# A gated mix of linear attention and a dense layer: dense units first, features laid out head by head, KV accumulated tile by tile

## The chip, the cores and the metric

One core of one Trainium2 chip. The metric is the device time of one execution in microseconds (us); lower is better. "Span" is the time from the first to the last instruction in a profile; in the runs below the time is 1.8 us longer than the span of the same execution. Engines are called by their names in the profile: PE (TensorE; PEld is its weight load), DVE (VectorE), ACT (ScalarE), POOL (GpSimd) and SP (which only issues transfers). A profile marks executions "slow" or "fast"; here one core runs alone, so "slow" only means over 1.5% above the fastest execution of that kernel.

## The reference, cut to what matters

```python
# x: 2048 x 512 (bf16).  H = 32 heads of 16.  DFF = 1376.
q, k, v  = split(x @ wqkv)                       # per head
pq, pk   = q @ w_phi[h], k @ w_phi[h]            # 16 x 16 per head
phi      = concat([softmax(p), softmax(-p)])     # 32 features per head
kv, z    = sum_s phi_k^T v, sum_s phi_k
a        = ((phi_q kv) / (phi_q z + 1e-6)) @ wo
b        = relu(x @ w1) @ w2
g        = sigmoid(sum(x * gate_w))
return g * a + (1 - g) * b
```

## The kernel before

Rows of x come in 16 tiles of 128. w_phi is folded into the q and k weights at the start (`WqP`, `WkP`), which needs those weights transposed. A *dense unit* is one product group of the dense layer: four 512-column matmuls and a relu; there are 44. The program order on PE is: fold, 16 tiles with the 44 units spread between them, a KV stage, and a final stage of 16 rounds (query product, B = hidden x w2, A = heads x wo). Softmax sums and reciprocals are DVE's, the scaling by them POOL's, the exponentials ACT's.

```python
# start: the transposed loads, one queue, wqkv first (SP); plain loads through POOL's software queue
S_wqk.op(lambda: sync.dma_start_transpose(out=WQKT, in_=A_wqkv[:, 0:2 * D]))
for q in range(NCH):
    S_xT[q].op(... sync.dma_start_transpose(out=XO[:, :, q*512:(q+1)*512], in_=x2[q*512:(q+1)*512, :]))
S_wv.op(lambda: pool.dma_start(out=WV[:, :, :], ...))
S_w1.op(lambda: pool.dma_start(out=W1[:, :, :], ...))
...
# PE, per tile: q and k features, V, and the gate as a one-column matmul
for dt in range(NDT):
    pe.matmul(PS[:, 0, :], lhsT, WqP[:, dt, :], ...); pe.matmul(PS[:, 1, :], lhsT, WkP[:, dt, :], ...)
for dt in range(NDT):
    pe.matmul(PS[:, 2, :], lhsT, WV[:, dt, :], ...);  pe.matmul(PS[:, 3, m:m + 1], lhsT, GW[:, dt, :], ...)
...
# PE, KV stage after all tiles: per group of 128 features, 16 tiles of (128 columns + 1 column for z)
pe.matmul(PS[:, kb, kc:kc + P], lhsT, VS[:, m, t*P:(t+1)*P], ...)
pe.matmul(PS[:, zb, zc:zc + 1], lhsT, ONES[:, 0:1], ...)
...
# PE, final stage: query product of 8 x 136 columns
pe.matmul(PS[:, bank, c0:c0 + P + 8], lhsT, KVNZ[:, g, :], ...)
```

The softmax here doesn't subtract the row's maximum and nothing guards it: scores larger than these inputs give would overflow.

## Time and profile before

Median 178.93 us of 3 runs (177.81 to 180.07). The head of the profile's page, with the chain of work that ended last:

```profile
span 176.5 us, 2702 instructions
...
PE 155.9 (88%) x1072; PEld 81.9 (46%) x1088; DVE 109.0 (62%) x197; ACT 70.0 (40%) x98; POOL 55.3 (31%) x49
...
PE 88%; DMA 5%; issue 2%; ACT 2%; DVE 1%
```

PE is on the chain for 88% of the span, so nearly every microsecond saved on PE should show. The window view of the same kernel, cut at five stages (each line: the stretch, its length, then busy time and number of instructions of PE, PEld, DVE, ACT, POOL, then the granted PE clock, the busy share of the DMA engines and their GB/s):

```profile
0.00:18.20 18.20, 3.61 (x33) 3.38 (x34) 3.90 (x10) 3.35 (x5) 5.30 (x14) 0.99 1.01 210
18.20:101.80 83.60, 82.38 (x423) 37.17 (x432) 71.34 (x96) 55.62 (x77) 49.01 (x35) 0.98 0.42 86
101.80:113.00 11.20, 10.50 (x257) 10.42 (x257) 5.38 (x27) 0.00 (x1) 0.99 (x1) 1.00 0.15 28
113.00:173.70 60.70, 59.40 (x361) 30.90 (x368) 27.71 (x64) 10.99 (x16) 0.00 (x0) 1.00 0.27 68
173.70:176.50 2.80, 0.00 (x0) 0.00 (x0) 0.72 (x1) 0.00 (x0) 0.00 (x0) 1.00 0.14 47
```

| stage | us | PE busy |
|---|---|---|
| start | 18.2 | 3.6 |
| tiles and dense units | 83.6 | 82.4 |
| KV | 11.2 | 10.5 |
| final stage | 60.7 | 59.4 |
| tail | 2.8 | 0 |

So the start is, but for the short tail, the only stage in which PE is mostly idle. The timeline (start, duration, engine, line, operation) says what it waits for: the transposed load of wqkv, issued at 0.75 and landed at 10.36.

```profile
0.75 3.98 SPq L226 DMA_TRANSPOSE HTW<-in_A_wqkv_dram  x1
...
10.36 1.89 PE L431 MATMUL PS<-Wbd,HTW 128*128 128x128 bf16 x16 [10.36 <-DMA HTW<-in_A_wqkv_dram]
```

The next lines, from the timeline of DVE and POOL inside one tile, show a place where DVE never idles. From one reciprocal (65.51) to the next (69.92) a tile takes DVE 4.41 us, and its small product at 67.56 (32 elements) ends at 68.11, just after POOL's multiply ends at 68.07:

```profile
65.51 0.55 DVE L363 RECIPROCAL SC<-ZB 128x64 f32<-128x64 f32 x1
...
66.14 1.93 POOL L279 TENSOR_TENSOR FM<-FM,SC 128x1024 bf16<-128x1024 bf16 x1 [2.20 <-DVE SC L363]
...
67.56 0.55 DVE L369 TENSOR_TENSOR SC<-ZB,SC 128x32 f32<-128x32 f32 x1
...
69.92 0.55 DVE L363 RECIPROCAL SC<-ZB 128x64 f32<-128x64 f32 x1
```

That the small product waits for POOL is plainer in the first tile, where POOL's multiply started late: there the same 32 elements took 1.75 us, and ended (28.72) just after POOL (28.66) once more.

```profile
26.72 1.94 POOL L279 TENSOR_TENSOR FM<-FM,SC 128x1024 bf16<-128x1024 bf16 x1
26.97 1.75 DVE L369 TENSOR_TENSOR SC<-ZB,SC 128x32 f32<-128x32 f32 x1
```

In the kernel before DVE's 4.41 us do not bind: a tile with its units takes PE 83.6 / 16 = 5.2 us.

### The profile page before, as it was taken

Reading aid. Unit: us, or ns where it says so; the run is one execution under the profiler, and the core shown is the slowest. Engines: PE = TensorE matmul, PEld = TensorE weight load, DVE = VectorE, ACT = ScalarE, POOL = GpSimd, SP = SyncE. Lnnn points to the kernel's source line nnn. Section 1 sums busy time; section 2 is a strip of 40 time slices with the busy share of each in tenths; the row PEclk is TensorE's granted clock in tenths of the full one; section 3 lists DMA queues with packets and bytes.
Section 4 is the critical chain, followed back from the end, with each engine's and each line's share of the span. In section 5 each row is a group of like instructions: output and inputs, shape, how many; then the busy total and the mean of one; then the engine's idle time right before and its main releaser. Section 6 shows DMA issues by size and latency. Waiting matters only on the chain.

```text
span 176.5 us, 2702 instructions
## 1 busy us (share of the span) xinstructions
PE 155.9 (88%) x1072; PEld 81.9 (46%) x1088; DVE 109.0 (62%) x197; ACT 70.0 (40%) x98; POOL 55.3 (31%) x49
## 2 busy tenths in 40 slices
PE   0061899999999999999999899799999999999993
PEld 0061344444444444444444399655555555555541
DVE  1223079988989889888899954444554445544431
ACT  2004067766666767666666700002111121111230
POOL 8300047666565446665566620000000000000000
PEclk9999699999999999999999999999999999999999
DMA  5999949933333320323333330041322232322321
GB/s 124 261 182 265 241 96 323 164 59 59 59 63 59 61 49 16 61 58 59 59 59 59 59 63 4 4 83 36 89 60 63 61 89 77 76 60 59 80 68 59
DMA packets 41467, 15.58 MB, mean 88 GB/s; under 512 B 38528, under 2 KB 40592, under 8 KB 41456
## 3 DMA queue, kind: packets, MB, share of 16 engines
q1 hardware_dynamic: 40352, 11.54, 32.8%
q0 software_dynamic: 1104, 3.88, 7.5%
q8 instruction: 8, 0.13, 0.3%
q14 instruction: 3, 0.02, 0.0%
HBM read 3.88 MB, written 2.10 MB: 34 GB/s over the span
## 4 chain that ended last, share of the span: by engine, by line
PE 88%; DMA 5%; issue 2%; ACT 2%; DVE 1%
PE PS L488 22%; PE PS L554 21%; PE PS L459 8%; PE PS L468 8%; PE PS L457 8%; PE PS L562 8%; PE PS L512 6%; DMA HTW<-in_A_wqkv_dram 5%; PE PS L539 4%; ACT WkP L295 1%; PE PS L431 1%; PE PS L437 1%; DVE OTM L412 0%; DVE OSB L421 0%; ACT HTW L317 0%
## 5 line engine op out<-in xcount | busy, mean ns | idle before, releaser
L488 PE MATMUL PS<-XO,W 128*128 128x512 bf16 (+1 forms) x171 | 40.3, 379 | 0.3
L554 PE MATMUL PS<-W,HTW 128*128 128x512 bf16 (+1 forms) x170 | 40.0, 379 | 0.3
L279 POOL TENSOR_TENSOR FM<-FM,SC 128x1024 bf16<-128x1024 bf16 x16 | 30.9, 1928 | 26.3 <-DVE SC L363 26.3
L327 ACT ACTIVATE TFA<-PS,GT 128x512 bf16<-128x512 f32 x16 | 11.0, 687 | 59.2 <-PE PS L562 42.0
L421 DVE SCALAR_TENSOR_TENSOR OSB<-PS,OMG,TFA 128x512 bf16<-128x512 f32 x16 | 12.0, 751 | 31.8 <-PE PS L554 20.8
L317 ACT ACTIVATE HTW<-PS 128x512 bf16<-128x512 f32 (+1 forms) x44 | 26.3, 598 | 7.5 <-PE PS L488 7.5
L457 PE MATMUL PS<-WqP,XO 128*128 128x512 bf16 x62 | 24.5, 395 | 4.2 <-issue 4.2
L309 ACT ACTIVATE FM<-PS 128x1024 bf16<-128x1024 f32 x16 | 16.4, 1023 | 22.6 <-PE PS L459 22.6
L459 PE MATMUL PS<-WkP,XO 128*128 128x512 bf16 x64 | 25.2, 393 | 0.1
L554 PEld LDWEIGHTS PS<-W,HTW 128*128 128x128 bf16 (+1 forms) x176 | 16.7, 98 | 17.5
L488 PEld LDWEIGHTS PS<-XO,W 128*128 128x128 bf16 (+1 forms) x176 | 15.4, 99 | 19.8 <-ACT HTW L317 3.8
L360 DVE TENSOR_REDUCE ZB<-FM 128x64 f32<-128x1024 bf16 x16 | 19.5, 1218 | 3.1 <-ACT FM L310 3.1
L364 DVE TENSOR_REDUCE ZB<-FM 128x64 f32<-128x1024 bf16 x16 | 18.6, 1161 | 0.0
L355 DVE CAST VS<-PS 128x512 bf16<-128x512 f32 x16 | 11.0, 686 | 10.8 <-PE PS L471 10.8
L285 POOL TENSOR_TENSOR FM<-FM,SC 128x512 bf16<-128x512 bf16 x16 | 16.9, 1055 | 2.0
L468 PE MATMUL PS<-WV,XO 128*128 128x512 bf16 x62 | 17.3, 377 | 0.0
L310 ACT ACTIVATE FM<-PS 128x1024 bf16<-128x1024 f32 x16 | 16.3, 1018 | 0.0
L562 PE MATMUL PS<-WO,XO 128*128 128x512 bf16 x63 | 16.2, 378 | 0.1
L412 DVE TENSOR_TENSOR OTM<-PS,RDEN 128x256 bf16<-128x256 f32 x32 | 12.1, 420 | 0.6
L457 PEld LDWEIGHTS PS<-WqP,XO 128*128 128x128 bf16 x64 | 6.4, 100 | 12.4 <-issue 5.3
L539 PE MATMUL PS<-KVNZ,PHQ 128*128 128x136 bf16 x128 | 10.0, 223 | 1.5 <-DVE OTM L412 0.9
L512 PE MATMUL PS<-VS,FM 128*128 128x128 bf16 x128 | 10.5, 216 | 0.8 <-ACT EG L320 0.8
(44 smaller groups left out, 134.7 us busy)
## 6 DMA issues: line engine op xcount, KB each, us to landing
out_dram<-OSB SPq DMA_DIRECT2D x16, 128.0 KB, 1.9
W<-in_B_w_dram POOLq DMA_DIRECT2D x1, 1376.0 KB, 12.7
W<-in_B_w_dram POOLq DMA_DIRECT2D x1, 1280.0 KB, 6.8
WV<-in_A_wqkv_dram POOLq DMA_DIRECT2D x1, 512.0 KB, 6.9
WO<-in_A_wo_dram POOLq DMA_DIRECT2D x1, 512.0 KB, 8.8
PHQ<-FM SPq DMA_TRANSPOSE x16, 3.1
XO<-OTM SPq DMA_TRANSPOSE x16, 2.4
W<-in_B_w_dram POOLq DMA_DIRECT2D x1, 96.0 KB, 6.5
```

What stands on the lines that cost most here:

```text
L279: POp.op(lambda m=m, b=b: pool.tensor_tensor(fmk(m).rearrange("p (g d) -> p g d", d=DH), fmk(m).rearrange("p (g d) -> p g d", d=DH), SC[:, ...
L317: ACp.op(lambda kt=kt, c=c, M=M, hb=hb: act.activation(HT[0:M, kt, c * 512:(c + 1) * 512], PS[0:M, hb, :], ACT.Relu), ev=f"rl{u}")
L360: VEp.op(lambda b=b, m=m: vec.tensor_reduce(ZB[:, b, 2 * H:4 * H], fmk(m).rearrange("p (g d) -> p g d", d=DH), AX.X, ALU.add), ev=f"zk{m}")
L364: VEp.op(lambda b=b, buf=buf: vec.tensor_reduce(ZB[:, b, 0:2 * H], fmq(buf).rearrange("p (g d) -> p g d", d=DH), AX.X, ALU.add), ev=f"zq{m}")
L457: PEp.op(lambda lhsT=lhsT, dt=dt, st=st, sp=sp: pe.matmul(PS[:, 0, :], lhsT, WqP[:, dt, :], start=st, stop=sp))
L459: PEp.op(lambda lhsT=lhsT, dt=dt, st=st, sp=sp: pe.matmul(PS[:, 1, :], lhsT, WkP[:, dt, :], start=st, stop=sp), ev=(f"pqk{m}" if sp else N ...
L468: PEp.op(lambda lhsT=lhsT, dt=dt, st=st, sp=sp: pe.matmul(PS[:, 2, :], lhsT, WV[:, dt, :], start=st, stop=sp), ev=(f"v{m}" if sp else None))
L488: PEp.op(lambda lhsT=lhsT, dt=dt, c=c, hb=hb, M=M: pe.matmul(PS[0:M, hb, :], lhsT, XO[:, dt, c * 512:(c + 1) * 512], start=(dt == 0), stop ...
L512: PEp.op(lambda lhsT=lhsT, kb=kb, kc=kc, m=m, t=t: pe.matmul(PS[:, kb, kc:kc + P], lhsT, VS[:, m, t * P:(t + 1) * P], start=(m == 0), stop ...
L539: PEp.op(lambda lhsT=lhsT, bank=bank, c0=c0, g=g, sg=sg: pe.matmul(PS[:, bank, c0:c0 + P + 8], lhsT, KVNZ[:, g, :], start=(sg == 0), stop= ...
L554: PEp.op(lambda kt=kt, M=M, m=m, B_b=B_b: pe.matmul(PS[:, B_b, :], HT[0:M, kt, m * P:(m + 1) * P], W2[0:M, kt, :], start=(kt == 0), stop=( ...
L562: PEp.op(lambda t=t, m=m, A_b=A_b: pe.matmul(PS[:, A_b, :], XO[:, t, m * P:(m + 1) * P], WO[:, t, :], start=(t == 0), stop=(t == NG - 1)))
```

## The change

The intent: fill PE's idle start with dense units, and take work off PE. The first 512 rows of x are loaded plainly and transposed on PE (after seven warm-up products), the first 8 dense units run while wqkv's transposed load is under way, and 3 more after the fold. Features are laid out head by head, so that a group of 128 features belongs to only 4 heads: products with V then need 64 columns plus one of ones, those with KV 68. KV is accumulated in PSUM three tiles behind the exponentials. The gate weights ride as a spare row of the last dense unit. Eleven units are kept for the time after the last tile. The diff, cut to its core:

```diff
+        WQKT = PHQ[:, :, S - 512:S]          # transposed wqkv in space for late query features
+        XS = OT[:, :, 0:512]
+        for j in range(4):                   # x0, plain, on two hardware queues
+            p.dma(("sp", "act")[j // 2], ... e.dma_start(out=XS[:, j, :], in_=x2[j * P:(j + 1) * P, :]), ...)
+        w1cuts = [0, 256, 512, 1024, DFF]
+        for i in range(4):                   # w1 in four cuts, ahead of wqkv
+            p.dma(("act", "act", "sp", "sp")[i], ... W1[:, :, a:b] ...)
+        p.wait("pool", ["x01", "x03"])
+        p.wait("sp", ["x03"])
+        p.dma("pool", ... out=WV[:, :, :] ...)                                # software queue
+        p.dma("sp", lambda e: e.dma_start_transpose(out=WQKT, in_=A_wqkv[:, 0:2 * D]), "wqk", ev="wqk")
+        for c in range(1, NCH):
+            p.dma("sp", ... e.dma_start_transpose(out=XT[:, :, c * 512:(c + 1) * 512], ...))
         ... cut ...
+        # per tile: q, k, V (no gate column); V waits for the cast of the tile before: one V bank
+                after=((["wv"] + ([f"cv{m - 1}"] if m else [])) if dt == 0 else ()), ...
+        # KV, three tiles behind: 8 products of 65 columns per tile
+                    PS[:, 6 + g // 4, (g % 4) * GW:(g % 4) * GW + 65],
+                    FM[:, b, 1, g * P:(g + 1) * P], VS[:, b, g, 0:65],
+        # query product: 8 products of 68 columns per tile
+                    PHQ[:, g, m * P:(m + 1) * P], KVNZ[:, g, :], start=True, stop=True),
-                        PS[:, 3, m:m + 1], lhsT, GW[:, dt, :], start=st, stop=sp),
-                    PS[:, kb, kc:kc + P], lhsT, VS[:, m, t * P:(t + 1) * P],
-                    PS[:, zb, zc:zc + 1], lhsT, ONES[:, 0:1],
-                                PS[:, bank, c0:c0 + P + 8], lhsT, KVNZ[:, g, :],
         ... cut ...
+        for kt in range(8):
+            hunit(0, kt)
+        pre()                                # the fold
+        for kt in range(8, KT):
+            hunit(0, kt)
+        # then 16 tiles with 22 units between them, 11 late units, the final stage
```

## The prediction

> **What bounds it now.** TensorE: the chain of waits gives PE 88% of the 176.5 us span, and the granted clock is 0.990. The windows and the timeline show five stages: start 18.2 us (10.4 of it waiting for the transposed load of wqkv, then products and copies); tiles plus dense units 83.6 (PE busy 82.4); KV 11.2; final stage 60.7 (PE busy 59.4); tail 2.8. Times run 2.4 us over the span.
>
> **Costs read from the timeline.** A 512-column matmul takes 0.2165 us in a stream, a 136-column one 0.059, a gate column adds 0.025 to 0.03, a KV pair (128+1 columns) 0.081 to 0.088. I estimate 0.04 for a 65- or 68-column matmul.
>
> **What the change does.**
> - Start: chunk 0 of x is loaded plainly and transposed on PE, so dense units fill the wait for wqkv. First unit at 6.5 us, wqkv still at 14, first tile at 19, but 11 of 44 units (9.5 us) are then done.
> - Gate column: 64 matmuls go, about 2 us.
> - KV: 256 matmuls in an own stage (11.2) become 128 short ones among the tiles, about 5 us.
> - Query product: 128 x 0.059 = 7.5 becomes about 5.
>
> **What takes over in the middle.** Per tile PE then needs 12 x 0.2165 + 22/16 units x 0.866 + 0.3 = 4.1 us on average (5.2 now). VectorE keeps its work per tile. The product of the scale waits for GpSimd: it ends 0.04 us after GpSimd's 1.93 us multiply. The Trainium skill, "SBUF — State Buffer", section "Who interferes with whom", says a tensor_tensor with both inputs in SBUF contends with GpSimd; this trace agrees. Where VectorE never idled (reciprocal at 65.51 to the next at 69.92) a tile took 4.41 us. Bank 2 is single: V of the next tile waits for VectorE's cast, in program order behind the previous tile's softmax sums. So VectorE can lag by little more than a us, and the tiles run at about 4.4 us, not 4.1: 16 tiles about 70 us. The exponentials' chain (1.93 + 1.94 us) stays just below. The 11 late units hide the last KV products: another 8.5 us.
>
> **Sum.** Start 19 + tiles and late units 79 (98) + final stage 16 x (2.38 + 0.87 + 0.3) = 57, plus about 2 us where it begins (first B waits for the last relu; first A waits for the transpose of the first numerator, 2.4 us) + tail 3.7 (A is last now) = 160.5 span, plus 2.4: **163 us**, 80% range 158 to 168.5. Faster by over 2% 0.96, within 0.03, slower 0.01.
>
> **What would show it right.** First dense matmul before 8 us, first tile at 17 to 21; tile period 4.3 to 4.6 us with VectorE over 90% busy in the tiles and PE waiting for the cast before V; no KV stage of its own; final period 3.5 to 3.6 us with PE over 95%; PE idle about 1 us at the final stage's start.
>
> **What would make it wrong.** VectorE less in the way: 4.1 us per tile, 158. Interleaved 16-element runs slowing the exponentials or GpSimd's multiply: a GpSimd or ScalarE period over 4.6 would add 3 to 10 us. GpSimd waits for the last x chunk (about 27 us) before it multiplies tile 0; counted as absorbed. A of the final stage now waits for a transpose only two tiles ahead, with 0.9 us of slack; a slower landing would stall every tile. wqkv could land 3 us later.

## The result, and the profile after

The changed kernel ran at a median of 170.57 us (4 runs, 168.54 to 172.73) against 178.39 us for the kernel before (4 runs). The ratio of fast runs is 0.953, 95% interval 0.944 to 0.962. Ratios in this document are the mean time of one kernel's fast runs over that of the other's of the same rounds, so not quite the ratio of the medians quoted. The kernel is faster, by about half of what was predicted, and 163 us with its range up to 168.5 missed.

The profile that came with this result fell in a slow execution (172.73 us). The kernel was therefore run again unedited (label `again`), and that profile is of a fast one (169.01 us). Its page:

```profile
span 167.2 us, 2373 instructions
...
PE 152.6 (91%) x919; PEld 72.3 (43%) x919; DVE 103.9 (62%) x174; ACT 72.9 (44%) x102; POOL 54.7 (33%) x48
...
PE 47%; DVE 33%; DMA 9%; issue 6%; ACT 2%; ACTq 1%; DVEq 0%
```

PE's busy time fell by only 3.3 us, though many products are gone: warm-up products (3.2 us) and transposes came in, and parts of the start ran at half clock. The chain changed its make-up: DVE, 1% of it before, is 33% of it now. The windows, cut at the first tile, the end of the dense units, and the last product:

```profile
0.00:26.30 26.30, 19.49 (x99) 9.37 (x100) 6.46 (x23) 9.26 (x15) 4.61 (x13) 0.87 1.03 188
26.30:105.60 79.30, 76.43 (x453) 35.60 (x452) 69.35 (x101) 52.64 (x71) 50.09 (x35) 1.00 0.35 80
105.60:163.90 58.30, 56.70 (x368) 27.35 (x368) 27.32 (x50) 10.74 (x16) 0.00 (x0) 1.00 0.30 71
163.90:167.20 3.30, 0.00 (x0) 0.00 (x0) 0.75 (x1) 0.26 (x1) 0.00 (x0) 0.83 0.12 40
```

| stage | predicted | fast run | off by |
|---|---|---|---|
| start, to the first tile | 19 | 26.3 | +7.3 |
| tiles and late units | 79 | 79.3 | +0.3 |
| final stage with its beginning | 57 + 2 | 58.3 | -0.7 |
| tail | 3.7 | 3.3 | -0.4 |
| time over span | 2.4 | 1.8 | -0.6 |
| time | 163 | 169.0 | +6.0 |

Each stage behind the first tile came out within a microsecond, though in the middle two errors cancelled (see the account at the end). The miss is in the start. Its timeline in the fast run (SPq is the issue on SP's queue):

```profile
4.24 14.46 SPq L170 DMA_TRANSPOSE PHQ<-in_A_wqkv_dram  x1
...
9.30 3.45 PE L223 MATMUL PS<-XT,W 128*128 128x512 bf16 x8 [3.22 <-DMA W<-in_B_w_dram]
14.87 7.04 PE L223 MATMUL PS<-XT,W 128*128 128x512 bf16 x24 [2.12 <-DMA W<-in_B_w_dram]
21.75 2.17 PE L253 MATMUL PS<-Wbd,PHQ 128*128 128x128 bf16 x32
...
26.34 0.38 PE L273 MATMUL PS<-WqP,XT 128*128 128x512 bf16 x1
```

Two kinds of losses are there. Units wait twice for w1 (3.22 and 2.12 us). And the products are slow for a while after each gap: 8 products in 3.45 us are 0.43 us each, while a stream at full clock takes 0.2165. The Trainium skill, "TensorE: Matmul & The Clock Gate", section "What's actually happening", says that an idle PE falls back to half its clock and needs a window of some 3.4 us of work to recover; this trace agrees with both. The view by windows of one microsecond gives a granted clock of 0.50 between 10 and 12 and between 16 and 19 us, and the windows beside them (0.54 and 0.75; 0.95 and 0.84) make each stretch some 3.4 us long. The second stretch begins a microsecond after PE had gone back to work at full pace, so the clock follows a gap with a delay.

The transposed load of wqkv, which the prediction worried about, held up nothing in this run: it landed at 20.9 us, while PE was at its units until 21.75. The chain that ended last, cut to the start, goes through w1's second cut instead, which was issued at 2.15 and landed at 14.82:

```profile
2.15 12.67 DMA W<-in_B_w_dram
...
14.87 7.04 PE PS L223 x24
```

In the slow run the start is longer, and there the fold itself waits for wqkv:

```profile
8.07 3.46 PE L223 MATMUL PS<-XT,W 128*128 128x512 bf16 x8 [2.19 <-DVE Wbd L200]
13.10 5.35 PE L223 MATMUL PS<-XT,W 128*128 128x512 bf16 x24 [1.57 <-DMA W<-in_B_w_dram]
23.06 3.59 PE L253 MATMUL PS<-Wbd,PHQ 128*128 128x128 bf16 x32 [4.61 <-DMA PHQ<-in_A_wqkv_dram]
...
30.15 0.38 PE L273 MATMUL PS<-WqP,XT 128*128 128x512 bf16 x1
```

Between these two executions the whole difference of 3.7 us lies before the first tile. That the scatter of the changed kernel over 4 us comes from there too is likely, but only these two were profiled. The loads behind it, from the list of transfers of the fast run (last figure: us from issue to landing):

```profile
WV<-in_A_wqkv_dram POOLq DMA_DIRECT2D x1, 512.0 KB, 13.1
...
PHQ<-in_A_wqkv_dram SPq DMA_TRANSPOSE x1, 16.7
```

The transposed load of wqkv takes 16.7 us (18.2 in the slow run), not the 9.6 us of before; it lands at 20.9 us. In the middle of the kernel DVE is as busy as foretold: it goes from one reciprocal to the next in 48.98 - 44.61 = 4.37 us with no idle time, and the cast of V (47.14) waits in program order behind the previous tile's sums:

```profile
44.61 0.55 DVE L297 RECIPROCAL SC<-ZB 128x64 f32<-128x64 f32 x1
...
46.66 0.56 DVE L304 TENSOR_TENSOR SC<-ZB,SC 128x32 f32<-128x32 f32 x1
47.14 0.68 DVE L291 CAST VS<-PS 128x512 bf16<-128x512 f32 x1
...
48.98 0.55 DVE L297 RECIPROCAL SC<-ZB 128x64 f32<-128x64 f32 x1
```

### The profile page after: what moved, and what is told of

Same layout as the page of the kernel before. It is cut to its first block, busy times and chain, and to the rows that moved or that the text cites. A ratio compares the mean times of both kernels' runs of the same rounds, so it can differ in the third digit from the quotient of the medians.

```text
span 170.9 us, 2373 instructions
## 1 busy us (share of the span) xinstructions
PE 153.3 (90%) x919; PEld 73.3 (43%) x919; DVE 104.2 (61%) x174; ACT 73.3 (43%) x102; POOL 54.6 (32%) x48
## 4 chain that ended last, share of the span: by engine, by line
PE 44%; DVE 32%; DMA 14%; issue 6%; ACT 2%; ACTq 0%; DVEq 0%
PE PS L384 21%; DMA PHQ<-in_A_wqkv_dram 11%; DVE ZB L294 9%; DVE ZB L299 9%; PE PS L223 9%; PE PS L394 8%; DVE VS L291 5%; DVE SC L302 3%; DMA OT<-in_A_x_dram 2%; PE PS L253 2%; PE PS L360 2%; DVE SC L297 2%; DVE SC L304 2%; DMA OT<-OTM 1%; ACT FM L288 1%
## 5 line engine op out<-in xcount | busy, mean ns | idle before, releaser
L223 PE MATMUL PS<-XT,W 128*128 128x512 bf16 (+1 forms) x176 | 44.3, 397 | 3.8 <-DVE Wbd L200 2.2
L384 PE MATMUL PS<-W,HT 128*128 128x512 bf16 (+1 forms) x176 | 40.6, 379 | 0.9 <-ACT EG L347 0.8
L288 ACT ACTIVATE FM<-PS 128x1024 bf16<-128x1024 f32 x32 | 31.0, 1021 | 20.6 <-PE PS L273 20.6
L237 ACT ACTIVATE HT<-PS 128x512 bf16<-128x512 f32 (+1 forms) x44 | 26.2, 598 | 16.9 <-PE PS L223 16.8
L223 PEld LDWEIGHTS PS<-XT,W 128*128 128x128 bf16 (+1 forms) x176 | 17.9, 104 | 25.5 <-issue 2.9
L273 PE MATMUL PS<-WqP,XT 128*128 128x512 bf16 x64 | 24.3, 380 | 1.0 <-ACT FM L288 0.6
L273 PE MATMUL PS<-WkP,XT 128*128 128x512 bf16 x64 | 24.2, 379 | 0.0
L384 PEld LDWEIGHTS PS<-W,HT 128*128 128x128 bf16 (+1 forms) x176 | 16.2, 97 | 18.7 <-issue 1.2
L299 DVE TENSOR_REDUCE ZB<-FM 128x64 f32<-128x1024 bf16 x16 | 18.6, 1161 | 0.0
L311 POOL TENSOR_TENSOR FM<-FM,SC 128x512 bf16<-128x512 bf16 x16 | 16.9, 1055 | 2.0
L279 PE MATMUL PS<-WV,XT 128*128 128x512 bf16 x64 | 16.5, 380 | 1.1 <-DVE VS L291 0.9
L394 PE MATMUL PS<-WO,OT 128*128 128x512 bf16 x64 | 16.4, 378 | 1.0 <-DMA OT<-OTM 1.0
L370 DVE TENSOR_TENSOR OTM<-PS,RDEN 128x512 bf16<-128x512 f32 x16 | 11.1, 692 | 0.5
```

The lines of the kernel that those rows point to most:

```text
L223: p.op("pe", lambda e, c=c, kt=kt, M=M, dt=dt, bank=bank: e.matmul(PS[0:M, bank, :], W1[:, dt, kt * P:kt * P + M], XT[:, dt, c * 512:(c + ...
L237: p.op("act", lambda e, c=c, kt=kt, Mr=Mr, bank=bank: e.activation(HT[0:Mr, kt, c * 512:(c + 1) * 512], PS[0:Mr, bank, :], ACT.Relu), afte ...
L273: p.op("pe", lambda e, m=m, dt=dt, which=which, W=W: e.matmul(PS[:, which, :], XT[:, dt, m * P:(m + 1) * P], W[:, dt, :], start=(dt == 0), ...
L279: p.op("pe", lambda e, m=m, dt=dt: e.matmul(PS[:, 2, :], XT[:, dt, m * P:(m + 1) * P], WV[:, dt, :], start=(dt == 0), stop=(dt == NDT - 1) ...
L288: p.op("act", lambda e, o=fm5[:, :, :, s, :], i=src, s=s: e.activation(o, i, ACT.Exp, scale=(1.0 if s == 0 else -1.0)), after=[f"qk{m}"] + ...
L299: p.op("dve", lambda e, b=b: e.tensor_reduce(ZB[:, b, 0:64], FM[:, b, 0, :].rearrange("p (g f) -> p g f", f=DH), AX.X, ALU.add), ev=f"zq{m}")
```

## The experiments

The question is why the loads of the start are slow. Three theories. A: the transposed load stands behind x0 and w1 in line, on DMA engines that are full anyway. B: traffic collapses while WV's plain load runs beside the transposed one. C: the new destination of the transposed load, eight pieces per partition with gaps, is slow to write. Each run states the edit against the changed kernel unless said otherwise. The runs came in three batches on three chips (`again` to `contig`; `wv_hw`, `both_late`, `cast_act`, `best1`; `before_hw`, `best2`, `best3`), each with the kernel before beside it, so runs of different batches are compared by their ratios or profiles.

### again: the changed kernel, unedited

> The changed kernel unedited, to get a profile of the fast state and the spread of its start. Every theory: ratio to the kernel before 0.95 to 0.96; the transposed load of wqkv lands at 20 to 23 us, the first tile starts at 27 to 30 us, tiles at 4.37 us each, final stage 3.5 us per tile.

Median 171.52 us (169.01 to 172.79; two of the four runs are slow, the two fast ones average 170.0), ratio 0.955 (0.946 to 0.965). In the profiled run the load landed at 20.9, as expected, and the first tile began at 26.3, a little earlier than expected.

### wv_late: WV only after wqkv has landed

```diff
-        p.wait("pool", ["x01", "x03"])
+        p.wait("pool", ["wqk"])
```

> WV is loaded only after the transposed load of wqkv has landed; nothing else changes. Theory A (the transposed load is slow because it stands behind x0 and w1 in line on full DMA engines): only the 0.5 MB of WV leave its way, it lands 2 to 3 us earlier, at about 20. Theory B (transposed traffic collapses from about 290 to about 85 GB/s while the software-queue load of WV runs beside it, from 12 to 20 us in the trace): it lands 5 to 8 us earlier, at 15 to 17, and the kernel gains 4 to 8 us. Theory C (the destination, eight strided pieces per partition instead of one run, makes it slow): no change of its rate.

Median 166.40 us, ratio 0.935 (0.930 to 0.941). All four runs are fast; their mean is 3.5 us below that of `again`'s fast runs, a little under the 4 to 8 us of theory B. In its list of transfers:

```profile
PHQ<-in_A_wqkv_dram SPq DMA_TRANSPOSE x1, 10.5
```

Issued at 4.38, landed at 14.9: six microseconds earlier for half a megabyte taken out of the way. That is theory B's landing, and twice theory A's gain. The time itself was won through w1: its second cut landed 9.1 us after its issue in place of 12.7, PE hardly waited for it (0.28 us at the weight load), and the first tile began at 22.6.

### w1_late: the two large w1 cuts behind wqkv

```diff
-        for i in range(4):
+        def w1load(i):
             ...
+        w1load(0)
+        w1load(1)
         ... transposed load of wqkv ...
+        w1load(2)
+        w1load(3)
```

> The two large cuts of w1 (0.85 MB) are put behind the transposed load of wqkv on the same queue. Theory A: the transposed load lands 5 to 7 us earlier, at 16 to 18; units 4 to 7 then wait for w1, so the first tile gains less, 2 to 5 us. Theory B: with WV still beside it, it stays slow, 18 to 22 us. Theory C: no change of its rate.

Median 174.01 us, ratio 0.975 (0.968 to 0.983): slower than `again`, which no theory had foreseen. wqkv landed 14.5 us after its issue at 4.13, at 18.6, in B's range and just past A's. And 0.85 MB taken out of its way gave 2 us, where the 0.5 MB of WV gave 6, so it is not the number of bytes ahead that counts. The first unit came earlier (6.9 us), and then PE stood (from the view of waits):

```profile
PE PS L227 <- DMA W<-in_B_w_dram: 9.2, 1, 9.2
```

### contig: a contiguous destination

```diff
-        WQKT = PHQ[:, :, S - 512:S]
+        WQKT = HT[:, 9:11, :].rearrange("p a (b d) -> p (a b) d", b=4)
```

> The transposed load of wqkv goes to one contiguous run of 8 KB per partition (space of hidden rows not yet written) as in the kernel before; queue order unchanged. Theory C: it lands near 4.8 + 9.6 = 14 us, the kernel gains 6 to 9 us. Theories A and B: it lands at 20 to 23 us as before, no gain over 1%.

Median 171.28 us, ratio 0.965 (0.958 to 0.972). The ratio is no sign of a loss: the two fast runs average 170.0 us, as in `again`. The load took as long as ever, so theory C falls:

```profile
HT<-in_A_wqkv_dram SPq DMA_TRANSPOSE x1, 17.2
```

### wv_hw: WV through a hardware queue

Same bytes, issued at much the same time (4.43), but from ACT's queue in place of POOL's. There WV stands in line behind the two small cuts of w1.

```diff
-        p.wait("pool", ["x01", "x03"])
+        p.wait("act", ["x01", "x03"])
-        p.dma("pool", lambda e: e.dma_start(     # WV
+        p.dma("act", lambda e: e.dma_start(
```

> WV is loaded at the same point as in the changed kernel (after x0), but through ScalarE's hardware queue in place of GpSimd's software queue. Theory B1 (what slows the rest is the software queue beside transposed traffic): the transposed load of wqkv lands at 15 to 17 us as with WV held back, and the kernel gains 3 to 6 us over the changed kernel (ratio about 0.93 to 0.94). Theory B2 (the 0.5 MB and the mixing of plain and transposed traffic as such): landing 19 to 22 us, ratio 0.95 to 0.96.

Median 165.15 us, ratio 0.931 (0.922 to 0.940). wqkv landed 12.9 us after issue, at 17.3 (just outside the range I had given B1), WV at 13.4, and the kernel gained as much as with WV held back. The transfer view over the same six microseconds (12 to 18 us) of the two kernels; q1 is SP's hardware queue with the transposed load, q0 POOL's software queue, q10 ACT's. First `again`:

```profile
DMA packets 1261, 0.48 MB, mean 80 GB/s; under 512 B 1204, under 2 KB 1220, under 8 KB 1261
...
q1 hardware_dynamic: 1196, 0.31, 103.3%
q0 software_dynamic: 47, 0.17, 16.7%
```

Then `wv_hw`:

```profile
DMA packets 5394, 1.46 MB, mean 243 GB/s; under 512 B 5277, under 2 KB 5394, under 8 KB 5394
...
q1 hardware_dynamic: 5265, 1.34, 114.7%
q10 hardware_dynamic: 129, 0.12, 5.7%
```

The engines are booked as busy in both, yet move 80 GB/s in one and 243 in the other. With WV in the software queue, 1196 transposed packets took nearly as much booked time as 5265 otherwise: they do not move, they stand. The chip is not the reason: `cast_act`, in the same batch as `wv_hw` but with WV in the software queue, moved 122 GB/s there, with 1085 transposed packets. But the window flatters `wv_hw`, where most of WV had moved by 12 us. And the edit changed more than the kind of queue: also WV's place in line, and its packets (0.12 MB in 129 of them, 0.17 MB in 47 before, so about 0.9 KB each in place of 3.6). Which of the three counts was not separated.

### both_late: the transposed load nearly alone

WV as in `wv_late`, w1 as in `w1_late`.

> WV and the two large cuts of w1 both wait behind the transposed load of wqkv, so that beside the last 0.5 MB of small w1 cuts it runs alone. A reading of its own rate: if it is bandwidth alone it lands about 5 us after issue, at 9 to 10 us (1 MB at some 290 GB/s, seen in the last part of the load once WV had landed). If the transposed load is slow by itself, at 13 or later. Units then wait for w1, so the time as a whole gains little: ratio 0.94 to 0.97.

One run, 166.46 us, state unknown. The load takes 6.5 us, of which the first part still shares with the small w1 cuts (landed at 11.1, a little later than the 9 to 10 expected). From the list, and from the transfer view between 8 and 10 us, when it is alone:

```profile
PHQ<-in_A_wqkv_dram SPq DMA_TRANSPOSE x1, 6.5
...
DMA packets 2267, 0.58 MB, mean 290 GB/s; under 512 B 2267, under 2 KB 2267, under 8 KB 2267
```

### before_hw: the kernel before with WV and w1 on a hardware queue

```diff
-            S_wv.op(lambda: pool.dma_start(...WV...))
-            S_w1.op(lambda: pool.dma_start(...W1...))
+            S_wv.op(lambda: act.dma_start(...WV...))     # at the head of ACT's program
+            S_w1.op(lambda: act.dma_start(...W1...))
```

> The kernel before, with WV and w1 (1.9 MB) loaded through ScalarE's hardware queue in place of GpSimd's software queue. If the software queue slows transposed traffic beside it (theory B1) there too, the transposed load of wqkv, first in its own queue, lands at 7 to 8.5 us in place of 10.4, and the kernel before gains 1 to 3 us (ratio 0.985 to 0.995). If it was only slow in the changed kernel because it stood behind w1 (theory A): no earlier landing, or a later one.

B1's half of this expectation failed; the result is the one named for theory A (which had fallen short in `w1_late`). Median 179.18 us, ratio 1.009 (1.001 to 1.018): no gain. The plain loads became fast (WV landed 4.2 us after issue), and the transposed load slower, 13.1 us in place of 9.6; the plain loads now moved before it (between 3 and 4 us 351 plain packets and 8 transposed ones) and beside it until 11.3 us:

```profile
WV<-in_A_wqkv_dram ACTq DMA_DIRECT2D x1, 512.0 KB, 4.2
...
HTW<-in_A_wqkv_dram SPq DMA_TRANSPOSE x1, 13.1
```

So "software queue beside transposed traffic is slow" is no general rule. In the kernel before, the transfer view between 4.8 and 10.4 us shows both kinds at 260 GB/s, though they mostly took turns: between 7 and 8 us 0.38 MB of plain packets and not one transposed. In `both_late`, WV in the software queue beside the transposed x moved 0.52 MB between 16 and 18 us, 316 GB/s in all. The slow case was seen in `again`, in `w1_late` (85 GB/s between 10 and 14 us) and, later and beside the transposed x, in `wv_late` (60 GB/s between 18.5 and 20.5). What brings it on is open.

One thing these views share: while a plain load moves fast, the transposed one moves little, whichever queue the plain one uses. In `before_hw` (hardware queue) the two moved the same number of packets, 98 and 98 between 6 and 7 us, 103 plain and 101 transposed between 7 and 8; but a plain packet there was about 2.7 KB and a transposed one 0.26 KB. In the kernel before (software queue) WV moved 0.51 MB between 6 and 8 us and the transposed load 0.07. What sets `again` apart is that the plain load is slow too: 0.17 MB of WV in six microseconds, so that the transposed load was held up for longer.

### cast_act: is DVE the limit of the tiles?

```diff
-            p.op("dve", lambda e, b=b: e.tensor_copy(
-                VS[:, b, :, 0:64], PS[:, 2, :].rearrange("p (g c) -> p g c", g=NG)),
+            p.op("act", lambda e, b=b: e.activation(
+                VS[:, b, :, 0:64], PS[:, 2, :].rearrange("p (g c) -> p g c", g=NG), ACT.Copy),
```

> The cast of V moves from VectorE to ScalarE; the start is left as it is. My theory of the tiles (VectorE's program order sets 4.37 us per tile, through the single V bank): the period falls to 4.05 to 4.15 us, PE's own need, VectorE gets idle time, and the kernel gains 3.5 to 5 us over the changed kernel (ratio 0.925 to 0.935). Rival (GpSimd's multiply or the exponentials' chain of 3.9 us, lengthened by the cast on ScalarE, set the period): it stays at 4.3 or more, no gain over 1%.

Median 167.81 us, ratio 0.945 (0.934 to 0.957), which overlaps `again`'s interval. In the profiles the first tile starts at the same place in both (26.3 and 26.4), and the span behind it falls from 140.9 to 139.2 us: 1.7 us, where 3.5 to 5 were expected. DVE left the chain, which became PE and ACT. From the views of waits between 26 and 90 us, first `again`, then `cast_act` (who waits, for whom, us in total, times, longest):

```profile
PE PS L279 <- DVE VS L291: 0.9, 2, 0.5
```

```profile
DVE ZB L294 <- ACT FM L288: 8.8, 6, 5.6
...
PE PS L273 <- ACT FM L288: 1.7, 6, 0.3
```

PE's wait for the cast is gone and DVE now idles for ACT, so the wait that the theory named was real. Its size was not what I had said: from the first to the last tile the mean period went from 4.22 to 4.13 us. DVE's 4.37 never became PE's mean, because PE could run ahead of DVE for the first tiles; the lag that it could build up is estimated from these at some 2.3 us (15 x (4.37 - 4.22)), not "little more than a us". Behind the cast, the exponentials were the next to be waited for, but for 1.7 us in all; at 4.13 us a tile, PE is near the 4.1 us that the prediction gave as its own need.

### best1, best2, best3: what the findings are worth together

`best1` holds WV back until wqkv has landed, issues all w1 cuts on ACT's queue, starts the transposed load after the first cut, and casts on ACT.

> Three edits at once, to beat both: WV after the transposed load; all w1 cuts on ScalarE's queue behind x0 and the transposed load only after the first cut; the cast of V on ScalarE. Expected: first dense unit at 6.5 to 7.5 us in place of 9.4, first tile at 20 to 22, tiles at 4.1 us, 158 to 161 us measured, ratio 0.89 to 0.905. If w1's later cuts starve beside the transposed load: first tile at 24 or later, ratio 0.91 to 0.92.

Median 162.63 us, ratio 0.909 (0.894 to 0.924): short of the range. In its profile, of a slow run, the first unit started at 8.4 us, not 7, and the 32 products of units 0 to 7 took 9.7 us up to the fold, where `best2` below takes 6.9. Much of that was at the pace of half clock, four products in a microsecond, though the profile has no record of a lowered clock there.

`best2` puts the loads in the order of need and none of the start's large ones on the software queue:

```diff
+        w1load(0)                # ACT's queue, behind x0
+        w1load(1)
         ...
-        p.wait("pool", ["x01", "x03"])
-        p.dma("pool", ... WV ...)
         p.wait("sp", ["x03"])
+        w1load(2)                # one line on SP: w1 cut 2, wqkv, w1 cut 3, WV, x1 to x3
         ... transposed load of wqkv ...
+        w1load(3)
+        p.dma("sp", ... WV ...)
```

> Cast of V on ScalarE, and all start loads on hardware queues in the order of need: x0 and two small w1 cuts, then on one queue w1 cut 2, wqkv transposed, w1 cut 3, WV, x1 to x3. Expected: first dense unit at 6.9 us as where the large w1 cuts came late, transposed load landed at 12 to 14, first tile at 19 to 20.5; span first tile plus 139.2 us as with the cast on ScalarE, so 158 to 160, measured 160.5 to 162.5, ratio 0.895 to 0.91. If some load comes late, PE waits in the start and the first tile is at 22 or later.

Median 159.58 us (159.30 to 159.94), ratio 0.901 (0.894 to 0.908): the time is 1 us better than foreseen, the first unit at 6.8, the first tile at 18.3 us, and the scatter is gone.

`best3` adds a few products against the clock gap and smooths where the final stage begins:

```diff
+        warm(4)                  # between the transposes and unit 0
         for kt in range(8):
             hunit(0, kt)
         ...
+            if i == 9:           # two late units still to come
+                kvfin()
+                gate()
+                nd(0)
             hunit(*u)
-        kvfin()
-        gate()
         finB(0)
-        nd(0)
-            after += [f"cb{m - 2}"] if m >= 2 else [f"rl{hcount[0] - 1}"]
+            after += [f"cb{m - 2}"] if m >= 2 else [f"rl{hcount[0] - 3 + 2 * m}"]
```

> As best2, plus four warm-up products between the transposes and the first unit (the units ran at 0.43 us per product after the gap), and the first query product moved before the last two dense units, the first B waiting only for the unit that used its bank. Expected: 1 to 2.5 us less at the start if the clock stays up, 1.5 to 2.5 us less where the final stage begins (PE idle there 0.8 + 0.8 + 0.4 us so far): 156 to 159 measured, ratio 0.875 to 0.89.

Median 157.78 us (157.37 to 158.67), ratio 0.891 (0.884 to 0.898; a hair above what was expected), the best of all, and correct. Its gain over `best2` was 0.5 us at the start and 1.4 at the final stage, both less than expected. At the final stage PE's waits of 0.78, 0.84 and 0.17 us in `best2` shrank to one of 0.16. At the start the four products can't take the credit: the 32 products of the first units took the same 7.08 us, at full clock, in `best2` without them; the units only began earlier, 6.31 in place of 6.76. Its page, and the first units from the timelines of `best2` and `best3`:

```profile
span 155.6 us, 2380 instructions
...
PE 148.8 (96%) x923; PEld 71.8 (46%) x923; DVE 97.2 (62%) x158; ACT 79.6 (51%) x118; POOL 53.9 (35%) x47
```

```profile
6.76 7.08 PE L226 MATMUL PS<-XT,W 128*128 128x512 bf16 x32 [0.60 <-DVE XT L200]
```

```profile
6.31 7.08 PE L226 MATMUL PS<-XT,W 128*128 128x512 bf16 x32
```

### The start against the rest

One table settles where the miss lies. For each profile: when the first tile starts, and how much of the span lies behind that. (In `both_late`, `wv_hw`, `cast_act` and `best1` the record of the first product is missing, and its start is taken 0.22 us before the next.)

| run | first tile, us | span, us | behind the first tile |
|---|---|---|---|
| with the result (slow) | 30.2 | 170.9 | 140.7 |
| again | 26.3 | 167.2 | 140.9 |
| contig | 26.4 | 167.1 | 140.7 |
| w1_late | 30.2 | 171.0 | 140.8 |
| both_late | 23.9 | 164.6 | 140.7 |
| wv_late | 22.6 | 163.9 | 141.3 |
| wv_hw | 22.5 | 163.3 | 140.8 |
| cast_act | 26.4 | 165.6 | 139.2 |
| best1 (slow) | 22.7 | 161.9 | 139.2 |
| best2 | 18.3 | 157.5 | 139.2 |
| best3 | 17.8 | 155.6 | 137.8 |

Seven profiles with the same middle have 140.7 to 141.3 us there; the prediction had 160.5 - 19 = 141.5. What moves between them is the start alone.

## Why the prediction was right or wrong

- **The step that failed: "First unit at 6.5 us, wqkv still at 14, first tile at 19".** Measured in the fast run: 9.3, 20.9 and 26.3. I took the 9.6 us of the transposed load from the trace of before and moved it to another place in time. But a transfer's duration is no property of the transfer. Before, this load was first in line; nearly alone, 1 MB takes 6.5 us (`both_late`); beside WV in the software queue it took 16.7. The term of the sum was "start 19", and it measured 26.3. The prediction named the danger ("wqkv could land 3 us later") and gave it less than half its size. It also had the wrong path: it let the start wait for wqkv, with units filling that wait. In the fast run PE waited for w1 instead, which the prediction left out. w1's first cut made the first unit late (9.3 us; 6.9 and 6.8 in `w1_late` and `best2`, where the large cuts were issued later), its second cut landed at 14.8, and each wait was followed by products at half clock. With the loads in the order of need (`best2`) the first tile came at 18.3, even before the 19 of the prediction.
- **The middle: the sum right, in part by luck.** Tiles and late units were predicted at 79 and took 79.3 us. DVE was busy 54.7 of 56 us between 32 and 88 us, 4.37 us per tile, and PE waited for the cast before V, as written. But the lag that DVE may have was understated, so PE's mean period was 4.22, not 4.4 and below the 4.3 to 4.6 that was to show the prediction right. From the first tile to the first late unit (94.65) it took 68.3 us where 70 were predicted; from there to the final stage 11.0 where 8.5 were, 0.8 of it a wait that the prediction booked under the final stage. The two errors cancelled.
- **Right: what PE is relieved of.** There is no KV stage any more. Eight 65-column products take about 0.25 us, 0.031 each; I had estimated 0.04. The final stage runs at 3.5 us per round (125.70 to 129.19 in the slow run's chain).
- **Right: the beginning of the final stage and the tail.** About 2 us were predicted for the first; PE waited 0.78 for the last relu and 0.85 and 0.16 for the first two transposes. The tail took 3.3 us.
- **Right: what was feared and did not come.** Interleaved 16-element runs cost nothing: an exponential took 1021 ns after, and 1023 or 1018 before, POOL's short multiply 1055 or 1059 after, and 1055 before. POOL waited for the last x chunk until 29.3 us and no one noticed. A's transpose came in time in every later round.
- **Where the expected gain went:** off the start's own account. The kernel before reaches its first tile at 18.2 us; the changed one at 26.3 or later, though with 11 units done. Had the first tile come at 19 and the rest stayed, this run's 169.0 would have been 161.7 (an estimate).

What stays open: why WV in the software queue crawls beside transposed traffic here (80 GB/s in all) and not in the kernel before (260 GB/s) or in `both_late` (316 GB/s).

## What to carry to other kernels

A load's time to landing, read from a trace, belongs to that trace's queue order: when a change moves loads in time, add up who shares the engines in each microsecond, and expect the start to be the most uncertain term. Put the loads of a start in one line in the order of need, and test a change of queue before a change of layout. And check a saved PE stage against the next engine's period, but count how far that engine may lag before it is felt.

## What the Trainium skill lacked or had wrong

- "DMA: Bandwidth & Descriptors", section "Queues, rings and completion order", says that each DMA engine goes round between its queues packet by packet. `before_hw` agrees (98 packets of each kind between 6 and 7 us). The page does not say that a plain load in the software queue can hold up a transposed load in a hardware queue: 80 GB/s together between 12 and 18 us, against 243 GB/s with the same plain load in another hardware queue (and by then mostly landed), and not always (316 GB/s in `both_late`).
- "SBUF — State Buffer", section "Who interferes with whom", gives one reason for a slow software-queue load: DVE holds the port that POOL needs to write descriptors. Here DVE ran nothing between 8.8 and 22.2 us while WV crept, so that reason does not cover this case. Its rule on a tensor_tensor with two SBUF inputs did fit: the small product ended 0.04 us after POOL's multiply (68.11 and 68.07), and took 1.75 us in place of 0.55 where that multiply started late.
- "DMA: Bandwidth & Descriptors", section "Latency and other measured facts", lists 261 GB/s for a transposed load with a non-contiguous middle dimension; alone, into strided pieces, this one ran at 290 GB/s over two microseconds. The page does not say over what its rate was taken, nor whether such pieces are its case.
- "TensorE: Matmul & The Clock Gate", section "Back-to-back issue gap", gives about 81 ns per product for a stream of weight load and 128-column matmul. Here 136-column products, each with its own weights, took 59 ns, and 65-column ones about 31 ns. The formula that the section gives for an isolated product, columns / 2.4 + 2.5 ns, comes to 59 and 30 ns and fits the stream better.
